# A means load over 128 partitions and long runs back from DRAM, in an attention kernel followed by a mixture of experts

## The chip, the cores and the metric

The kernel runs on one core of one Trainium2 chip. The metric is device time in microseconds. A profiled execution gives its own time, and beside it a span, from the first to the last instruction, with a record of every instruction and every DMA packet.

## The reference

Two parts, one after the other. The attention works on `q`, `k`, `v` of 8 batches, 8 heads, 576 positions and 64 features. The change sits in its first half, an attention between means of four neighbouring positions:

```python
q_d = q.reshape(B, H, Sd, factor, D).mean(axis=3)     # Sd = 144, factor = 4
k_d, v_d = ...                                        # likewise
out_d = sm_attn(q_d, k_d, v_d)                        # softmax attention, 144 x 144 a head
out_up = np.repeat(out_d, factor, axis=2)             # each row serves four positions
...
out_local = np.matmul(attn, v)                        # positions nearer than 4
return (out_up + out_local).astype(np.float32)
```

The result, as 4,608 tokens of 512 features, goes to a mixture of 16 experts in 4 groups: a group is chosen for a token, an expert in the group, and that expert's two layers (512 to 1,024, ReLU, back to 512) are applied and weighted.

## The kernel before

**Units.** The attention is done in 16 units. A unit is two heads of two batches: the two heads lie on partitions 0 to 63 and 64 to 127 of `q` and `k`, the two batches along the row. Values are laid out by the host in two forms: `vw`, windows of 42 positions for the local part, and `vm`, groups of four positions side by side for the means.

**Order.** All steps of all units are written out by hand in one long list (`ORDER`), and each engine runs its own instructions in that order. So a step that waits holds up everything behind it on the same engine. Most loads and the store and load of `odd` are issued on SP, in the order of the list; stores of `x` on ScalarE's queue.

**Means.** `pool_q` and `pool_k` add four positions of `q` and `k` (one VectorE reduction, or three GpSimd adds; the last letter of the step says which). `load_v` loads a unit's `vm` with two DMAs: 112 partitions with two chunks of 2 KB each (keys 0 to 111 of the one head, 32 to 143 of the other), and 64 partitions with one chunk (32 keys of each head). There are three buffers `vs`, and `clear vs i` sets partitions 64 to 111 of the third chunk to zero once. `pool_v` adds the four positions to `vd`.

**Attention of the means.** `s_down` multiplies `q` and `k` means into `b_d`, `s_down_exp` makes `Pd` of it, `turn_pd` transposes `Pd` on TensorE in three parts (by key chunk), `turn_pd_out` copies these to `PdT`, `out_down` multiplies by `vd`, `turn_down` turns the product back and `turn_down_out` divides by the sums, into `odn`.

**The way back through DRAM.** `down_store` writes `odn` to a DRAM buffer `odd` (two buffers), 512 bytes a row for two heads. `load_down` reads it back into 8 partitions of the window buffer `vw` of the unit, row `8l + r` to partition `2 + 15r`, place `l`: 256 bytes at a time. There these rows lie among the values of the windows, so that one multiplication in `x_bank` (L446) adds both halves of the attention. `turn_x`, `logits`, the router's steps and `store_x` follow.

**After the attention** the router's lists are finished, tokens are gathered, and the experts run one after another with weights that are loaded and split in the same rhythm, TensorE being the engine that sets it.

Of the kernel before, what the change touches and what calls it, by code (L numbers as in the profile page):

```python
# [9 lines left out]
F32 = mybir.dt.float32  # L10
# [4 lines left out]
ALU = mybir.AluOpType  # L15
AX = mybir.AxisListType
# [3 lines left out]
P = 128  # L20
B, H, S, D = 8, 8, 576, 64
SD = S // 4
G = 9
# [23 lines left out]
NATURAL = 2  # L47
HALVES = (slice(0, 5), slice(5, G))

KEYS = ((slice(0, 112), 112), (slice(112, 176), 64), (slice(176, 288), 112))  # L50

TILES = (slice(0, P), slice(160, 160 + P), slice(112, 176))

# [1 line left out]
class Attention:  # L55
# [9 lines left out]
    def __init__(self, tc, q, k, vm, vw, idf, xd, left, right, dram):  # L65
        nc = self.nc = tc.nc
        self.tc, self.q, self.k, self.vm_in, self.vw_in, self.idf = tc, q, k, vm, vw, idf
        cp = self.cp = left.enter_context(tc.tile_pool(name="attc", bufs=1))
        self.a1 = left.enter_context(tc.tile_pool(name="att1", bufs=1))
        self.a2 = left.enter_context(tc.tile_pool(name="att2", bufs=2))  # L70
        self.inp = right.enter_context(tc.tile_pool(name="inp", bufs=2, side="right"))
        self.odd = [dram.tile([320, P], F32, name=f"odd{i}") for i in range(2)]
        self.st, self.banks, self.lg = {}, {}, {}
        self.turns = 0
        self.xd = xd
        self.kt = [self.inp.tile([P, 2, S], F32, name=f"kt{i}", bufs=1) for i in range(3)]
        self.kz = [self.inp.tile([P, 2, 2, S + 6], F32, name=f"kz{i}", bufs=1) for i in range(2)]
        self.load_k(0)
        self.load_q(0)
        self.mask = self.inp.tile([P, G, W], BF16, name="mask", bufs=1)  # L80
        self.vw = [(cp if i < 2 else self.inp).tile([P, 2, 2 * NBLK, D], F32, name=f"vw{i}", bufs=1) for i in range(3)]
        self.warm = self.inp.tile([P, 4 * P], BF16, name="warm", bufs=1)
        nc.vector.memset(self.warm, 0.0)
        one = cp.tile([1, 1], F32, name="one")
        nc.gpsimd.memset(one, 0.0)
        nc.scalar.activation(one, one, AF.Exp)
        self.zero = cp.tile([P, 1], F32, name="zero")
        nc.gpsimd.memset(self.zero, 0.0)
        self.idb = cp.tile([P, P], BF16, name="idb")
        self.vd = [self.inp.tile([112, 3, 2, D], F32, name=f"vd{i}", bufs=1) for i in range(2)]  # L90
        self.vs = [self.inp.tile([112, 3, 2, 4 * D], F32, name=f"vs{i}", bufs=1) for i in range(3)]
        self.mg = [cp.tile([P, 5], F32, name=f"mg{i}") for i in range(2)]
        self.sg = [cp.tile([P, 5], F32, name=f"sg{i}") for i in range(2)]
        self.rg = [cp.tile([P, 6], F32, name=f"rg{i}") for i in range(2)]
        self.kept = {}
        for n, more, shape in (
            ("pt", 1, [P, G * P]), ("x", 2, [P, G, P]), ("PdT", 1, [112, 3, 2 * SD]), ("od", 1, [P, 2 * SD]), ("odn", 1, [P, 3, 2, D])
        ):
            self.kept[n] = [cp.tile(shape, F32, name=f"{n}0")] + [self.inp.tile(shape, F32, name=f"{n}{i + 1}", bufs=1) for i in range(more)]
        self.E = [cp.tile([P, G, WW, 3], F32, name=f"E{i}") for i in range(2)]  # L100
        self.shares = self.inp.tile([P, 8], F32, name="shares", bufs=1)
        self.xT = cp.tile([P, 27 * P // 2], F32, name="xT")
        self.edge = self.inp.tile([P, 3, W], F32, name="edge", bufs=1)
# [9 lines left out]
    def clear(self, what, i):  # L113

        memset = self.nc.gpsimd.memset
        if what == "E":
            for w, c in ((slice(0, LEAD), slice(0, 3)), (slice(LEAD + W, WW), slice(0, 3)), (slice(LEAD, LEAD + W), slice(2, 3))):
                memset(self.E[i][:, :, w, c], 0.0)
            self.nc.gpsimd.tensor_copy(self.E[i][:, :, 0:40:5, 2], self.shares.unsqueeze(1).to_broadcast([P, G, 8]))
        elif what == "kz":  # L120
            memset(self.kz[i][0:64, 1], 0.0)
            memset(self.kz[i][64:P, 0], 0.0)
            for c in (slice(0, 3), slice(3 + S, 6 + S)):
                memset(self.kz[i][:, :, :, c], 0.0)
        else:
            memset(self.vs[i][64:112, 2], 0.0)

    def masks(self):

# [63 lines left out]

    def load_v(self, u):
        vs = self.vs[u % 3].rearrange("p c b x -> p c (b x)")
        self.nc.sync.dma_start(out=vs[:, 0:2], in_=self.vm_in[u, :, 0:2])
        self.nc.sync.dma_start(out=vs[0:64, 2], in_=self.vm_in[u, 0:64, 2])

    def load_windows(self, u):

# [5 lines left out]
    def pool_q(self, u, eng):  # L206
        s = self.st[u]
        s["qd"] = self.inp.tile([P, 2 * SD], F32, tag="qd", name=f"qd{u}")
        x = s["qT"].rearrange("p b (s t) -> p (b s) t", t=4)
        if eng == "D":  # L210
            self.nc.vector.tensor_reduce(out=s["qd"], in_=x, axis=AX.X, op=ALU.add)
        else:
            self.add4(s["qd"], [x[:, :, t] for t in range(4)])

    def add4(self, o, x):
        nc = self.nc
# [92 lines left out]
    def s_down(self, u):  # L309
# [18 lines left out]
        for h, r in enumerate(hs):  # L328
            for b in range(2):
                o = rest[64 * h + 32 * b : 64 * h + 32 * b + 32]  # L330
                q = qd[r, 112 + 32 * b : 144 + 32 * b]
                if h == 0:
                    mm(o, q, kd[r, b])
                else:
                    mm(o[:, 0:112], q, kd[r, b, 32:])
                    mm(o[:, 112:], q, kd[r, b, :32])

    def s_down_max(self, u):
        V = self.nc.vector
# [31 lines left out]

    def turn_pd(self, u, kc):

        pt = self.bank(("pd", kc), u, [P, 2 * SD + P])
        lo = KEYS[kc][0].start
        pd = self.st[u]["Pd"]
        tr = self.nc.tensor.transpose
        if kc == 1:
            tr(pt[:, 2 * SD :], pd[:, 4, SD - P :], self.idf)
        else:  # L380
            o = 112 - 32 * kc
            tr(pt[:112, o : o + P], pd[:, 4, 0:112], self.idf)
        for b in range(2):
            n = P if kc == 1 else 112
            tr(pt[:n, 160 * b : 160 * b + P], pd[:, 2 * b : 2 * b + 2].rearrange("p h s -> p (h s)")[:, lo : lo + n], self.idf)

    def turn_pd_out(self, u, kc, eng):
        s = self.st[u]
        s["PdT"] = self.of("PdT", u)
        pt = self.banks.pop((("pd", kc), u))  # L390
        o = s["PdT"][:, kc]
        if kc == 1:
            two = lambda x: x.rearrange("p (b s) -> p b s", b=2)[:, :, 0:P]
            self.evac(eng, two(s["PdT"][:64, kc : kc + 2].rearrange("p k s -> p (k s)")[:, 0:320]), two(pt[:64, 0:320]))
            for h in range(2):
                self.evac(eng, o[32 * h : 32 * h + 32, 112:176], pt[96:, 2 * SD + 64 * h : 2 * SD + 64 * h + 64])
        else:
            self.evac(eng, o, pt[:112, 0 : 2 * SD])

    def out_down(self, u):  # L400
        nc = self.nc
        vd, pdt = self.vd[u % 2], self.st[u]["PdT"]
        pt = self.bank("od", u, [P, 2, SD])
        for r, kc, o in ((slice(0, 112), 0, 0), (slice(0, 112), 2, 64), (slice(0, 32), 1, 0), (slice(32, 64), 1, 64)):
            for b in range(2):
                nc.tensor.matmul(
                    pt[o : o + 64, b], vd[r, (0, 2, 1)[kc], b], pdt[r, kc, SD * b : SD * b + SD], start=(kc != 1 and b == 0), stop=(kc == 1), skip_group_check=True
# [22 lines left out]

    def down_store(self, u, q):

        o, d = self.of("odn", u).rearrange("p c h d -> p c (h d)"), self.odd[u % 2]
        self.queue(q).dma_start(out=d.rearrange("(c p) d -> p c d", c=2)[0:P], in_=o[:, 0:2])
        self.queue(q).dma_start(out=d[P:160], in_=o[16:48, 2])

    def load_down(self, u, q):

        self.queue(q).dma_start(out=self.windows(u)[2:ROWS:15][0:8], in_=self.odd[u % 2][0 : 2 * SD].rearrange("(l r) (h d) -> r h l d", r=8, h=2))

    def x_bank(self, u, i):
        pt = self.bank(("x", i), u, [P, 3, P])
# [773 lines left out]


ORDER = """
shared_rows; warm_up 12; masks; masks_out A; clear_windows 0; load_k 1; clear E 1; s_local 0 1; pool_q 0 D; pool_k 0 D; clear E 0; load_q 1
s_local 0 0; s_local_out 0 1; quarter_sum; clear vs 0; s_local_out 0 0; load_k 2; load_q 2; pool_q 1 P; load_v 0; s_down 0; warm_up 6  # L1220
s_down_max 0; s_local_exp 0 1; s_down_exp 0 0; s_local_exp 0 0; s_down_exp 0 2; s_down_exp 0 1; pool_q 2 D; pool_k 1 D; s_local 1 1
s_local_out 1 1; s_local 1 0; spread 2 0 A; spread 2 1 P; clear kz 0; pool_v 0; clear kz 1; clear vs 2; clear vs 1; pool_k 2 P; turn_pd 0 0
s_local_out 1 0; soft_local_sum 0 D; turn_pd 0 2; load_k 3; turn_pd 0 1; turn_pd_out 0 1 A; turn_pd_out 0 0 A; soft_local 0
turn_pd_out 0 2 A; s_down 1; s_local_exp 1 0; out_down 0; s_local_exp 1 1; turn_e 0 0; s_down_max 1; turn_e 0 2; s_down_exp 1 0
soft_down 0 D; s_down_exp 1 1; s_down_exp 1 2; clear_windows 1; load_windows 0; turn_e 0 1; out_down_out 0 D; soft_local_sum 1 D
turn_e_out 0 2 A; s_local 2 1; s_local_out 2 1; load_q 3; constants; load_k 4; s_local 2 0; spread 3 0 A; spread 3 1 P; turn_e_out 0 0 A
# [207 lines left out]
```

## Time and profile before

| what | value |
| --- | --- |
| runs (three): lowest, median, highest | 739.65, 745.89, 752.54 us |
| profiled execution: its own time | 742.23 us |
| its span | 740.3 us |
| mean granted TensorE clock | 0.975 |
| TensorE (PE) busy, share of the span | 696.6 us, 94% |
| VectorE (DVE), ScalarE (ACT), GpSimd (POOL) busy | 460.4, 388.1, 254.8 us |
| DMA | 144.94 MB, mean 196 GB/s |

A busy engine is one with an instruction in it; TensorE's matmuls are pipelined, so busy does not mean at its peak. The busy shares are means over two very different stages, the attention and the experts, so stretches are to be read one by one. A wait is put down to what came last, and an instruction that waits holds up its engine's queue.

### The profile page before, as it was taken

The page shows a single profiled execution, that of the slowest core. Times are in us where ns is not written, and L with a number is a line of the kernel's source. Part 1 is how long each engine was busy: PE and PEld are TensorE (multiplying, and loading weights), DVE is VectorE, ACT ScalarE, POOL GpSimd, SP SyncE. Part 2 cuts the span into 40 slices and gives each one's busy share as a digit, 9 for nine tenths or more (in the row PEclk, how much of TensorE's full clock was granted, in tenths as well). Part 3 has the DMA queues.
Part 4 walks back from the last instruction along what each step waited for, and adds up shares of the span by engine and source line. Part 5 has one row for each costly group of instructions (what it writes and reads, how often), then busy time and mean ns, then how long its engine had stood idle before and what let it go on. Part 6 is the DMA issues. An engine that isn't in the chain of part 4 may idle for free. (4 is left out here: it accounts for less than half of the span.)

```text
span 740.3 us, 17944 instructions
## 1 busy us (share of the span) xinstructions
PE 696.6 (94%) x7135; PEld 627.9 (85%) x7135; DVE 460.4 (62%) x821; ACT 388.1 (52%) x830; POOL 254.8 (34%) x301
## 2 busy tenths in 40 slices
PE   7789987988986989999999999999999999999997
PEld 4666766766765868998999999999999999999996
DVE  5777987979984756654445555464555555565641
ACT  6767744857674316653444444454554554555531
POOL 7956655558634732002211120312203213212211
PEclk7889998999999999999999999999999999999999
DMA  9979899999978456846554555556655665656600
GB/s 292 250 176 238 259 265 240 237 234 272 234 212 234 114 176 207 273 131 197 156 171 143 166 188 172 191 158 204 188 172 191 212 198 189 226 186 203 222 27 26
DMA packets 109911, 144.94 MB, mean 196 GB/s; under 512 B 22736, under 2 KB 78544, under 8 KB 109824
## 3 DMA queue, kind: packets, MB, share of 16 engines
q1 hardware_dynamic: 85216, 113.25, 52.7%
q0 software_dynamic: 7088, 21.66, 8.5%
q10 hardware_dynamic: 17520, 8.85, 4.9%
q8 instruction: 57, 0.93, 0.5%
q14 instruction: 30, 0.25, 0.1%
HBM read 122.43 MB, written 22.29 MB: 195 GB/s over the span
## 5 line engine op out<-in xcount | busy, mean ns | idle before, releaser
L885 PE MATMUL ph<-xh,w1h 128*128 128x256 f32 (+13 forms) x512 | 161.1, 316 | 0.0
L856 POOL DMA_INDIRECT xg<-xd,gi x47 | 48.6, 1034 | 323.0 <-ACT yo L959 290.3
L885 PE MATMUL ph<-xl,w1h 128*128 128x256 f32 (+13 forms) x512 | 156.1, 306 | 0.0
L885 PE MATMUL ph<-xh,w1l 128*128 128x256 f32 (+13 forms) x512 | 156.0, 307 | 0.0
L844 DVE TENSOR_TENSOR w2l<-raww,w2h 128x1024 fp32r<-128x1024 f32 x61 | 74.6, 1224 | 73.7 <-ACT w2h L843 63.3
L933 PE MATMUL y<-hl,w2h 128*128 128x416 f32 (+11 forms) x384 | 115.3, 311 | 0.0
L933 PE MATMUL y<-hh,w2l 128*128 128x416 f32 (+11 forms) x384 | 114.3, 308 | 0.0
L843 ACT ACTIVATE w2h<-raww 128x1024 fp32r<-128x1024 f32 x64 | 67.6, 1058 | 73.5 <-PE y L933 54.0
L885 PEld LDWEIGHTS ph<-xh,w1h 128*128 128x128 f32 x512 | 96.2, 188 | 1.4 <-issue 0.2
L885 PEld LDWEIGHTS ph<-xl,w1h 128*128 128x128 f32 x512 | 96.3, 188 | 0.9
L844 DVE TENSOR_TENSOR w1l<-raww,w1h 128x1024 fp32r<-128x1024 f32 x60 | 73.4, 1224 | 38.1 <-ACT w1h L843 32.8
L885 PEld LDWEIGHTS ph<-xh,w1l 128*128 128x128 f32 x512 | 96.2, 188 | 0.3
L890 DVE SCALAR_TENSOR_TENSOR hl<-ph,hh 128x256 fp32r<-128x256 f32 (+13 forms) x128 | 60.3, 476 | 55.5 <-ACT hh L889 52.6
L889 ACT ACTIVATE hh<-ph 128x256 fp32r<-128x256 f32 (+13 forms) x128 | 53.9, 422 | 71.9 <-PE ph L885 65.9
L933 PE MATMUL y<-hh,w2h 128*128 128x416 f32 (+11 forms) x384 | 87.7, 312 | 0.0
L843 ACT ACTIVATE w1h<-raww 128x1024 fp32r<-128x1024 f32 x64 | 67.6, 1058 | 31.0 <-PE ph L885 24.2
L933 PEld LDWEIGHTS y<-hh,w2l 128*128 128x128 f32 x384 | 72.3, 188 | 0.1
L933 PEld LDWEIGHTS y<-hl,w2h 128*128 128x128 f32 x384 | 72.2, 188 | 0.1
L960 POOL DMA_INDIRECT out_dram<-yo,oi x47 | 47.9, 1020 | 65.5 <-ACT yo L959 51.9
L933 PEld LDWEIGHTS y<-hh,w2h 128*128 128x128 f32 x384 | 62.9, 188 | 0.1
L446 PE MATMUL b_x<-vw,pt 126*32 126x128 f32 x1152 | 40.9, 285 | 9.5 <-DMA vw<-odd 5.1
L865 ACT ACTIVATE xh<-xt 128x256 fp32r<-128x256 f32 (+14 forms) x68 | 27.0, 420 | 39.8 <-PE xt L872 39.8
(227 smaller groups left out, 1289.0 us busy)
## 6 DMA issues: line engine op xcount, KB each, us to landing
raww<-in_moe_w_dram SPq DMA_DIRECT2D x128, 512.0 KB
vw<-in_vw_dram SPq DMA_DIRECT2D x32, 378.0 KB
kt<-in_k_dram SPq DMA_DIRECT2D x16, 576.0 KB
qT<-in_q_dram SPq DMA_DIRECT2D x16, 576.0 KB
xd<-x ACTq DMA_DIRECT2D x15, 576.0 KB
vs<-in_vm_dram SPq DMA_DIRECT2D x16, 448.0 KB
vw<-odd SPq DMA_DIRECT2D x16, 144.0 KB
vs<-in_vm_dram SPq DMA_DIRECT2D x16, 128.0 KB
```

The source lines that it names most:

```text
L446: self.nc.tensor.matmul(pt[32 * j : 32 * j + 32, t], self.of("pt", u)[:ROWS, 32 * lin : 32 * lin + 32], self.windows(u)[:ROWS, :, lin], st ...
L843: self.nc.scalar.activation(hi, raw, AF.Copy)
L844: eng.tensor_tensor(out=lo, in0=raw, in1=hi.bitcast(F32), op=ALU.subtract)
L856: self.nc.gpsimd.indirect_dma_start(out=xg[:w], out_offset=None, in_=self.xd[0:rows], in_offset=bass.IndirectOffsetOnAxis(ap=st["gi"][:w, ...
L865: self.nc.scalar.activation(hi, x, AF.Copy)
L885: nc.tensor.matmul(ph, a[:, k, cs], st[b][:, k], start=(n == 0), stop=(n == 11))
L889: nc.scalar.activation(hh, ph, AF.Relu)
L890: nc.vector.scalar_tensor_tensor(out=hl, in0=ph, scalar=0.0, in1=hh.bitcast(F32), op0=ALU.max, op1=ALU.subtract)
L933: nc.tensor.matmul(y, a[:, f % 2, cs], b, start=(f == 0 and n == 0), stop=(f == 7 and n == 2))
L960: i = nc.gpsimd.indirect_dma_start(out=self.out, out_offset=bass.IndirectOffsetOnAxis(ap=oi, axis=0), in_=yo[:m], in_offset=None, bounds_c ...
```

## The change

The means' keys are cut differently: keys 0 to 127 of the one head and 16 to 143 of the other in the two large chunks, so that the first load fills 128 partitions, and 16 keys of each head in the small one, loaded to partitions 48 to 79. The buffers `vs`, `vd` and `PdT` get 128 partitions. The third chunk of `vs` is now cleared as a whole, before anything is loaded, and these clears stand earlier in the order; the copy `quarter_sum` takes the place of two of them. The host lays out `vm` as two contiguous blocks a unit. `turn_pd` makes one transpose more for the middle part, `s_down` needs one multiplication where it took two for the second head. `pool_q` writes its means in the order batch, row within a block, block, instead of batch, block, row; the rows of `odd` then come in that order, with one head after the other, and `load_down` reads runs of 18 rows (4,608 bytes) instead of single ones of 256 bytes. `down_store` writes 256 bytes a row and head, with three DMAs instead of two.

The core of the diff (the sizes of buffers and the indices that follow from the new cut are left out):

```diff
-KEYS = ((slice(0, 112), 112), (slice(112, 176), 64), (slice(176, 288), 112))
+FIRST = (0, 80, 160)
+MAIN = P * 2 * 8 * D
...
-        self.odd = [dram.tile([320, P], F32, name=f"odd{i}") for i in range(2)]
+        self.odd = [dram.tile([2, 2 * SD, D], F32, name=f"odd{i}") for i in range(2)]
...
-            memset(self.vs[i][64:112, 2], 0.0)
+            memset(self.vs[i][:, 2], 0.0)
...
-        self.nc.sync.dma_start(out=vs[:, 0:2], in_=self.vm_in[u, :, 0:2])
-        self.nc.sync.dma_start(out=vs[0:64, 2], in_=self.vm_in[u, 0:64, 2])
+        self.nc.sync.dma_start(out=vs[:, 0:2], in_=self.vm_in[u, 0:MAIN].rearrange("(p c x) -> p c x", p=P, c=2))
+        self.nc.sync.dma_start(out=vs[48:80, 2], in_=self.vm_in[u, MAIN:].rearrange("(p x) -> p x", p=32))
...
-        x = s["qT"].rearrange("p b (s t) -> p (b s) t", t=4)
+        o = s["qd"].rearrange("p (b r k) -> p b r k", b=2, r=8)
+        x = s["qT"].rearrange("p b (k r t) -> p b r k t", r=8, t=4)
         if eng == "D":
-            self.nc.vector.tensor_reduce(out=s["qd"], in_=x, axis=AX.X, op=ALU.add)
+            self.nc.vector.tensor_reduce(out=o, in_=x, axis=AX.X, op=ALU.add)
         else:
-            self.add4(s["qd"], [x[:, :, t] for t in range(4)])
+            self.add4(o, [x[:, :, :, :, t] for t in range(4)])
...
-                if h == 0:
-                    mm(o, q, kd[r, b])
-                else:
-                    mm(o[:, 0:112], q, kd[r, b, 32:])
-                    mm(o[:, 112:], q, kd[r, b, :32])
+                mm(o, q, kd[r, b])
...
         if kc == 1:
-            tr(pt[:, 2 * SD :], pd[:, 4, SD - P :], self.idf)
+            tr(pt[:, 224 : 224 + P], pd[:, 4, 0:P], self.idf)
+            tr(pt[:, 352 : 352 + P], pd[:, 4, SD - P :], self.idf)
...
-        o, d = self.of("odn", u).rearrange("p c h d -> p c (h d)"), self.odd[u % 2]
-        self.queue(q).dma_start(out=d.rearrange("(c p) d -> p c d", c=2)[0:P], in_=o[:, 0:2])
-        self.queue(q).dma_start(out=d[P:160], in_=o[16:48, 2])
+        o, d = self.of("odn", u), self.odd[u % 2]
+        for c in range(2):
+            self.queue(q).dma_start(out=d[:, 160 * c : 160 * c + P].rearrange("h p d -> p h d"), in_=o[:, c])
+        self.queue(q).dma_start(out=d[:, P:160].rearrange("h p d -> p h d"), in_=o[16:48, 2])
...
-        self.queue(q).dma_start(out=self.windows(u)[2:ROWS:15][0:8], in_=self.odd[u % 2][0 : 2 * SD].rearrange("(l r) (h d) -> r h l d", r=8, h=2))
+        t = self.windows(u)[2:ROWS:15][0:8].rearrange("p h (b k) d -> p (h b) (k d)", b=2)
+        self.queue(q).dma_start(out=t, in_=self.odd[u % 2].rearrange("h (b r k) d -> r (h b) (k d)", b=2, r=8))
...
-shared_rows; warm_up 12; masks; masks_out A; clear_windows 0; load_k 1; clear E 1; s_local 0 1; pool_q 0 D; pool_k 0 D; clear E 0; load_q 1
-s_local 0 0; s_local_out 0 1; quarter_sum; clear vs 0; s_local_out 0 0; load_k 2; load_q 2; pool_q 1 P; load_v 0; s_down 0; warm_up 6
+shared_rows; warm_up 12; masks; clear vs 0; masks_out A; clear_windows 0; load_k 1; clear E 1; s_local 0 1; pool_q 0 D; pool_k 0 D
+clear E 0; clear vs 1; clear vs 2; load_q 1; s_local 0 0; s_local_out 0 1; s_local_out 0 0; load_k 2; load_q 2; pool_q 1 P; load_v 0
...
-s_local_out 1 1; s_local 1 0; spread 2 0 A; spread 2 1 P; clear kz 0; pool_v 0; clear kz 1; clear vs 2; clear vs 1; pool_k 2 P; turn_pd 0 0
+s_local 1 1; s_local_out 1 1; s_local 1 0; spread 2 0 A; spread 2 1 P; clear kz 0; pool_v 0; clear kz 1; quarter_sum; pool_k 2 P
...
-    laid["vm"] = _np.stack([mean[:, 0:112], mean[:, 176:288], mean[:, 112:224]], axis=2)
+    main = _np.stack([mean[:, 0:P], mean[:, 160:288]], axis=2)
+    laid["vm"] = _np.concatenate([x.reshape(4 * NB, -1) for x in (main, mean[:, P:160])], axis=1)
```

## Rows read from the trace of the kernel before

**Rows 1.** stretches: us, engines' busy us (instructions), granted clock, DMA share, GB/s

```profile
0.00:220.00 220.00, 191.56 (x3574) 143.43 (x3575) 177.92 (x390) 146.12 (x430) 138.74 (x199) 0.94 0.93 243
...
300.00:700.00 400.00, 400.00 (x2779) 393.91 (x2778) 220.56 (x304) 197.52 (x316) 78.22 (x77) 1.00 0.59 188
```

**Rows 2.** TensorE's waits, 0 to 226 us: total us, times, longest us

```profile
PE b_s L265 <- ACT Pd L353: 5.8, 5, 3.7
PE b_x L446 <- DMA vw<-odd: 5.1, 2, 2.9
```

**Rows 3.** timeline, TensorE and ScalarE, 112 to 120 us: start, us, what, idle before

```profile
118.18 0.48 PE L265 MATMUL b_s<-mask,idb 128*128 128x380 bf16 x1 [3.68 <-ACT Pd L353]
...
116.27 0.49 ACT L166 ACTIVATE x<-b_x 128x384 f32<-128x384 f32 x1 [4.08 <-DMA xd<-x]
```

**Rows 4.** table of stretches, around the stall at 113 us

```profile
113.00:118.00 5.00, 1.50 (x23) 1.10 (x21) 0.86 (x1) 1.64 (x7) 4.53 (x7) 0.89 0.83 226
117.00:124.00 7.00, 5.82 (x86) 4.43 (x85) 6.56 (x14) 4.79 (x17) 4.46 (x5) 0.52 1.00 268
```

**Rows 5.** DMA view, 4 to 10 us: loads of k and q alone

```profile
DMA packets 583, 2.39 MB, mean 399 GB/s; under 512 B 64, under 2 KB 64, under 8 KB 583
...
q1 hardware_dynamic: 583, 2.39, 100.2%
```

**Rows 6.** DMA view, 45 to 46 us: a means load almost alone

```profile
DMA packets 108, 0.34 MB, mean 340 GB/s; under 512 B 13, under 2 KB 13, under 8 KB 108
```

**Rows 7.** DMA view, 11 to 15 us: a means load among others

```profile
DMA packets 309, 1.03 MB, mean 257 GB/s; under 512 B 41, under 2 KB 41, under 8 KB 309
```

**Rows 8.** DMA view, 23 to 27 us: a means load among others

```profile
DMA packets 282, 0.86 MB, mean 214 GB/s; under 512 B 41, under 2 KB 41, under 8 KB 282
```

**Rows 9.** DMA view, 43 to 44 us: odd's load alone (40 slices)

```profile
DMA  0000000000000000003344544655475565645644
...
DMA packets 267, 0.07 MB, mean 68 GB/s; under 512 B 267, under 2 KB 267, under 8 KB 267
...
q1 hardware_dynamic: 267, 0.07, 29.4%
```

**Rows 10.** DMA view, 84 to 85 us: store of odd alone

```profile
DMA packets 139, 0.06 MB, mean 57 GB/s; under 512 B 28, under 2 KB 139, under 8 KB 139
...
q1 hardware_dynamic: 139, 0.06, 21.8%
```

**Rows 11.** DMA view, 214 to 215 us: a store of 16 bytes a run

```profile
DMA packets 783, 0.01 MB, mean 13 GB/s; under 512 B 783, under 2 KB 783, under 8 KB 783
...
q1 hardware_dynamic: 783, 0.01, 36.1%
```

**Rows 12.** waits of SP's queue, 0 to 226 us

```profile
SPq L439 <- DMA odd<-odn: 34.9, 12, 7.5
```

**Rows 13.** timeline of SP's queue, 30 to 48 us

```profile
33.45 0.41 SPq L435 DMA_DIRECT2D odd<-odn  x1
...
41.99 0.69 SPq L439 DMA_DIRECT2D vw<-odd  x1
```

**Rows 14.** timeline, GpSimd, 0 to 120 us

```profile
4.76 0.31 POOL L119 COPY E<-shares 128x72 f32<-128x72 f32 x1
...
5.90 0.94 POOL L551 COPY quarters<-idf 32x32 f32<-32x32 f32 x4
...
9.55 0.69 POOL L217 TENSOR_TENSOR qd<-qT 128x288 f32<-128x288 f32 x1 [2.13 <-DMA qT<-in_q_dram]
...
22.19 0.99 POOL L126 MEMSET vs<- 48x512 f32 x2
```

**Rows 15.** timeline, TensorE, 0 to 60 us

```profile
30.37 0.38 PE L385 MATMUL b_pd<-idf,Pd 128*112 128x128 f32 x2
...
33.27 1.16 PE L316 MATMUL b_d<-kd,qd 64*128 64x144 f32 x20
```

**Rows 16.** instructions on qd: duration ns min/median/max

```profile
L218 POOL TENSOR_TENSOR qd<-qd,qT x9: 934/952/1458, 10.3 to 178.5; 128x288 f32<-128x288 f32 x9
```

More of the change, by code (lines that the diff above doesn't have):

```diff
@@ L89, in __init__ @@
         self.idb = cp.tile([P, P], BF16, name="idb")
-        self.vd = [self.inp.tile([112, 3, 2, D], F32, name=f"vd{i}", bufs=1) for i in range(2)]
-        self.vs = [self.inp.tile([112, 3, 2, 4 * D], F32, name=f"vs{i}", bufs=1) for i in range(3)]
+        self.vd = [self.inp.tile([P, 3, 2, D], F32, name=f"vd{i}", bufs=1) for i in range(2)]
+        self.vs = [self.inp.tile([P, 3, 2, 4 * D], F32, name=f"vs{i}", bufs=1) for i in range(3)]
         self.mg = [cp.tile([P, 5], F32, name=f"mg{i}") for i in range(2)]
@@ L96, in __init__ @@
         for n, more, shape in (
-            ("pt", 1, [P, G * P]), ("x", 2, [P, G, P]), ("PdT", 1, [112, 3, 2 * SD]), ("od", 1, [P, 2 * SD]), ("odn", 1, [P, 3, 2, D])
+            ("pt", 1, [P, G * P]), ("x", 2, [P, G, P]), ("PdT", 1, [P, 3, 2 * SD]), ("od", 1, [P, 2 * SD]), ("odn", 1, [P, 3, 2, D])
         ):
@@ L372, in turn_pd @@
     def turn_pd(self, u, kc):
-        pt = self.bank(("pd", kc), u, [P, 2 * SD + P])
-        lo = KEYS[kc][0].start
+        pt = self.bank(("pd", kc), u, [P, 2 * SD + 3 * 64])
+        lo = FIRST[kc]
         pd = self.st[u]["Pd"]
@@ L378, in turn_pd @@
         if kc == 1:
-            tr(pt[:, 2 * SD :], pd[:, 4, SD - P :], self.idf)
+            tr(pt[:, 224 : 224 + P], pd[:, 4, 0:P], self.idf)
+            tr(pt[:, 352 : 352 + P], pd[:, 4, SD - P :], self.idf)
         else:
             o = 112 - 32 * kc
-            tr(pt[:112, o : o + P], pd[:, 4, 0:112], self.idf)
+            tr(pt[:, o : o + P], pd[:, 4, 8 * kc : 8 * kc + P], self.idf)
         for b in range(2):
-            n = P if kc == 1 else 112
-            tr(pt[:n, 160 * b : 160 * b + P], pd[:, 2 * b : 2 * b + 2].rearrange("p h s -> p (h s)")[:, lo : lo + n], self.idf)
+            tr(pt[:, 160 * b : 160 * b + P], pd[:, 2 * b : 2 * b + 2].rearrange("p h s -> p (h s)")[:, lo : lo + P], self.idf)
     def turn_pd_out(self, u, kc, eng):
@@ L393, in turn_pd_out @@
             two = lambda x: x.rearrange("p (b s) -> p b s", b=2)[:, :, 0:P]
-            self.evac(eng, two(s["PdT"][:64, kc : kc + 2].rearrange("p k s -> p (k s)")[:, 0:320]), two(pt[:64, 0:320]))
+            self.evac(eng, two(s["PdT"][:, kc : kc + 2].rearrange("p k s -> p (k s)")[:, 0:320]), two(pt[:, 0:320]))
             for h in range(2):
-                self.evac(eng, o[32 * h : 32 * h + 32, 112:176], pt[96:, 2 * SD + 64 * h : 2 * SD + 64 * h + 64])
+                self.evac(eng, o[64 * h : 64 * h + 64, 112:176], pt[64 - 64 * h : P - 64 * h, 352 - 64 * h : 416 - 64 * h])
         else:
-            self.evac(eng, o, pt[:112, 0 : 2 * SD])
+            self.evac(eng, o, pt[:, 0 : 2 * SD])
     def out_down(self, u):
@@ L403, in out_down @@
         pt = self.bank("od", u, [P, 2, SD])
-        for r, kc, o in ((slice(0, 112), 0, 0), (slice(0, 112), 2, 64), (slice(0, 32), 1, 0), (slice(32, 64), 1, 64)):
+        for r, kc, o in ((slice(0, P), 0, 0), (slice(0, P), 2, 64), (slice(0, 64), 1, 0), (slice(64, P), 1, 64)):
             for b in range(2):
@@ L1218 @@
 ORDER = """
-shared_rows; warm_up 12; masks; masks_out A; clear_windows 0; load_k 1; clear E 1; s_local 0 1; pool_q 0 D; pool_k 0 D; clear E 0; load_q 1
-s_local 0 0; s_local_out 0 1; quarter_sum; clear vs 0; s_local_out 0 0; load_k 2; load_q 2; pool_q 1 P; load_v 0; s_down 0; warm_up 6
-s_down_max 0; s_local_exp 0 1; s_down_exp 0 0; s_local_exp 0 0; s_down_exp 0 2; s_down_exp 0 1; pool_q 2 D; pool_k 1 D; s_local 1 1
-s_local_out 1 1; s_local 1 0; spread 2 0 A; spread 2 1 P; clear kz 0; pool_v 0; clear kz 1; clear vs 2; clear vs 1; pool_k 2 P; turn_pd 0 0
-s_local_out 1 0; soft_local_sum 0 D; turn_pd 0 2; load_k 3; turn_pd 0 1; turn_pd_out 0 1 A; turn_pd_out 0 0 A; soft_local 0
+shared_rows; warm_up 12; masks; clear vs 0; masks_out A; clear_windows 0; load_k 1; clear E 1; s_local 0 1; pool_q 0 D; pool_k 0 D
+clear E 0; clear vs 1; clear vs 2; load_q 1; s_local 0 0; s_local_out 0 1; s_local_out 0 0; load_k 2; load_q 2; pool_q 1 P; load_v 0
+s_down 0; warm_up 6; s_down_max 0; s_local_exp 0 1; s_down_exp 0 0; s_local_exp 0 0; s_down_exp 0 2; s_down_exp 0 1; pool_q 2 D; pool_k 1 D
+s_local 1 1; s_local_out 1 1; s_local 1 0; spread 2 0 A; spread 2 1 P; clear kz 0; pool_v 0; clear kz 1; quarter_sum; pool_k 2 P
+turn_pd 0 0; s_local_out 1 0; soft_local_sum 0 D; turn_pd 0 2; load_k 3; turn_pd 0 1; turn_pd_out 0 1 A; turn_pd_out 0 0 A; soft_local 0
 turn_pd_out 0 2 A; s_down 1; s_local_exp 1 0; out_down 0; s_local_exp 1 1; turn_e 0 0; s_down_max 1; turn_e 0 2; s_down_exp 1 0
```

## The prediction

> **What bounds the kernel now.** I read the table of stretches first [rows 1]. From 300 to 700 us TensorE is busy in every microsecond of the 400, and the change touches nothing there; that part can only begin earlier or later. The attention, which the change edits, fills the first 220 us. There TensorE is busy 191.6 us, so 28.4 us of it are idle, and the DMA engines are busy for 0.93 of the time while they move only 243 GB/s. So two things press on this stage at once, and what it can win is some of those 28.4 us.
>
> Second, TensorE's waits in that stage [rows 2]. Two name the transfers: 5.1 us for `vw<-odd` (the rows that come back from DRAM), and the 3.7 us wait inside the 5.8 us for `Pd`. The second is a transfer in disguise, as the timeline of the two engines shows [rows 3]: the score matmuls of L265 stand still until 118.18 us for ScalarE's exponentials, and ScalarE itself had stood for 4.08 us until 116.27 us, because it could not overwrite `x` before an older store of it had landed. [...] Together 5.1 + 3.7 + 2.9 = 11.7 us: this is the ceiling of what faster transfers can give, if every transfer wait went. The rest of the idle time (the start, the clears on ScalarE, waits on VectorE) is not the transfers' and stays.
>
> Third, what a transfer costs. Loads of `k` and `q` alone run at 399 GB/s with all engines busy [rows 5]. A means load almost alone runs at 340 GB/s [rows 6]. Where it lies among other loads the engines are just as busy, but only 257 GB/s [rows 7] or 214 GB/s [rows 8] come through.
>
> **The means load (128 partitions).** It moves 576 KB (590 kB) a unit before and after, 448 + 128 KB then, 512 + 64 KB now. Time of a unit now: 590/340 = 1.73 us almost alone, 590/257 = 2.30 us and 590/214 = 2.76 us among others. If the new shape ran like `k` and `q`, it would take 590/399 = 1.48 us. The gain is thus between 0.25 and 1.28 us a unit. Below nothing: the small part now goes to 32 partitions, and the narrowest load in the trace, the rows to 8 partitions, makes 8 x 256 / 17.6 ns = 116 GB/s (worked out below) [rows 9]. At that the 65.5 kB take 0.56 us, and with the 524 kB at 340 (1.54 us) that is 2.10 us, a loss of 0.37 us against 1.73. I take a gain of 0.4 us, nearer to the lone row than to the crowded ones, since the crowd (window loads, the 512-byte stores of `x`) is not changed. 16 units: 6.4 us of all DMA engines' time; ends 5.9 us lost and 20.5 us gained.
>
> What speaks against a gain here is that a partition of the large part receives 4,096 bytes before and after, and one of the small part 2,048. [...]
>
> **The rows from DRAM.** Now one load is 576 runs of 256 bytes. A run costs 0.294 x 16 x 1,000 / 267 = 17.6 ns, and in the later slices about half of the 16 engines work [rows 9]; eight partitions, eight engines, 72 runs each: 1.27 us. After, an engine has 4 runs of 4,608 bytes. Such a run costs 1.002 x 16 x 6,000 / 519 = 185 ns, the 64 tiny packets of that view left out [rows 5]: 0.74 us. Gain 0.53 us of eight engines, 0.27 us of all, a unit; 4.3 us in all. If the runs were cut into small ones again, nothing.
>
> The store pays. 288 runs of 512 bytes become 576 of 256, and two issues become three. A stored run of 512 bytes costs 0.218 x 16 x 1,000 / 139 = 25 ns, 31 if the 28 tiny ones cost nothing [rows 10]. No row stores 256 bytes: the nearest are a stored run of 16 bytes, 0.361 x 16 x 1,000 / 783 = 7.4 ns [rows 11], and a loaded one of 256, 17.6 ns. I take 17.6 (same size; the 16-byte store shows that a short store is not dear in itself): 576 x 17.6 / 16 = 0.63 us against 288 x 28 / 16 = 0.50, so +0.13 us. Ends: 7.4 ns, -0.24 us; 31 ns, the price of a run twice as long, +0.62 us. 16 units: +2.1 us (-3.8 to +9.9).
>
> [...]
>
> **The queue.** SP issues the load behind the stores, and waits for them at its head: 34.9 us in 12 waits [rows 12]. In unit 0 the second store was issued at 33.45 us and the load went out at 41.99, and until then SP could issue nothing else: the means loads, `k`, `q` and windows behind it wait too [rows 13]. The third store adds one issue of 0.41 us (that of the second, in the same rows) and 0.13 us of writing ahead of that wait, the load itself gives 0.53 us back. Net for the chain store, load, L446: nothing.
>
> **What costs nothing, and its cover.** GpSimd: the clear of `vs` 0 moves ahead of the clears of `E`, those of `vs` 1 and 2 ahead of the first `qd` add, which now begins at 9.55 us after 2.13 us of waiting for `qT`; the two (0.99 us) fit there, while the copy of `quarters` (0.94 us) leaves that place and takes theirs at 22.19 us [rows 14]. Without that cover it would be 1 us once. A clear of 128 partitions costs what one of 48 does, since it has the same 512 elements in a row. The small means load of unit 0 now waits for that clear, on SP, some 0.3 us; nothing is queued behind it until 9.07 us. TensorE: one transpose more a unit, at most 0.38/2 = 0.19 us (two in 0.38 us), and four matmuls in `s_down` become two, 2 x 1.16/20 = 0.12 us less [rows 15]: at most 16 x 0.07 = 1 us, in a stage with 28 us idle. Evacuations and means keep their elements a partition; taller operands (128 for 112, 64 for 32 rows) change no length. `pool_q` reads with a step of 128 bytes instead of 16. Nine of 16 are on GpSimd, three adds each. Bounds: nothing, as elements are the same; or the price of the copy into `E`, whose runs are as short, 0.31 us for 72 elements, 4.3 ns each [rows 14], which would make 1.24 us of an add that now takes 0.95 [rows 16]: 27 x 0.29 = 8 us. GpSimd is idle 81 of the 220 us [rows 1], so I take nothing.
>
> **Sum.** DMA work a unit: -0.4 - 0.27 + 0.13 = -0.54 us, 8.6 us in all, of 0.93 x 220 = 205 us. The slack of the DMA engines goes from 7 to 11%. I estimate that time spent waiting in a line goes with one over its slack, so about 1 - 7/11 = 0.36, say 0.4, of the 11.7 us should go: 4.7 us. What goes next to the front is TensorE's own order: it is busy 87% of this stage already, and waits on the other engines remain. The profiled execution took 742.23 us (740.3 span, 1.9 around it): 737.5. The runs' median is 745.89, with 739.65 and 752.54 as the others; on that scale 741.2. I write 739.5, between the two.
>
> **Rivals.** *No gain:* the means load is as fast as its bytes a partition, its term is nothing, and 4.3 - 2.1 = 2.2 us of DMA work are left, a slack of 8% and 0.12 of 11.7 us: 1.4 us, 741 (744.5 on the median's scale). For it: 340 GB/s alone. Against: 214 and 257 among others. That the long runs don't come about, or that the strided adds eat them, ends in the same place, 742. *All of it:* the crowded rows are the means load's own doing, the term is +20 us, slack 17%, and the waits and the slow clock go: -11.7, 730.5. Against: `x` stores and window loads crowd too. *Slower:* SP's head of line. If stored runs of 256 bytes cost what 512 do, each unit holds SP 0.41 + 0.62 = 1.03 us longer, and everything queued behind starts that much later: 16.5 us over 16 units. With the same share reaching TensorE as above, 0.4, it is +6.6 us, 749. It decides from the point where the stores grow by more than the 0.53 us that the load saves.
>
> **How the numbers follow.** Forecast 0.47; no gain 0.29; all of it 0.12; slower 0.12. The forecast's own range is 2 to 9 us less (733 to 740, up to 744 on the median's scale). Runs of one kernel here spread by 13 us, so a difference below 2% is about what a measurement cannot tell from none, and the range reaches to 730 and to 750. Faster by over 2% means below 731: 0.10, the best half of "all of it" and some spread. Slower by over 2% means above 760.8: 0.03. Within: 0.87.
>
> **What would show it.** Right: the share of DMA time over the first 220 us falls below 0.9; windows with a means load show well over 257 GB/s; the rows' load goes from 576 packets to a few dozen of 4,608 bytes; `vw<-odd` nearly leaves TensorE's waits; and the expert stage begins 4 to 5 us earlier. Wrong: the same 214 to 257 GB/s in those windows; more than 34.9 us of SP waiting for `odd`; GpSimd adds on `qd` over 1.2 us; or an attention that shortens its waits and gets others in their place, since each engine keeps to its written order.

## The result and the profile after

The changed kernel takes 734.99 us (median of 6 runs, 733.48 to 737.93); beside it the kernel before took 745.72 (6 runs, 739.65 to 757.93). The ratio is 0.9859 [0.9819, 0.9900]: faster, by less than 2%. The profiled execution took 734.79 us with a span of 732.8, against 742.23 and 740.3. The forecast was 739.5 with a range of 730 to 750. It expected 4.7 us less; the medians lie 10.7 us apart, the profiled executions 7.4. On two other chips, below, the medians lie 11.2 and 6.1 us apart. The ratios leave out every run more than 1.5% above the fastest of its kernel, which on the chip of the first four experiments takes 15 of the 35 runs of before (the median of the rest is 740.13 us, not 742.91) and none of the others', so that those four ratios lie 0.4 to 0.6% above the ratios of the medians.

Where did the time go? First the end of the attention: the last matmul of L446 starts at 237.4 us before and at 228.8 after. The table of stretches up to these points, before and then after (us, busy us of TensorE, weight load, VectorE, ScalarE and GpSimd with their instructions, granted clock, DMA share, GB/s); the fence of after also has the stretches that answer [rows 1] and [rows 4]:

```profile
0.00:237.40 237.40, 203.41 (x3766) 152.03 (x3770) 186.09 (x411) 152.25 (x443) 144.58 (x203) 0.94 0.92 243
...
30.00:40.00 10.00, 7.22 (x108) 5.67 (x108) 8.29 (x18) 9.12 (x26) 9.46 (x10) 1.00 1.03 250
```

```profile
0.00:228.80 228.80, 202.05 (x3721) 148.60 (x3722) 186.44 (x411) 152.16 (x444) 145.37 (x203) 0.95 0.85 253
...
0.00:220.00 220.00, 195.27 (x3633) 144.09 (x3634) 184.18 (x406) 148.60 (x437) 140.68 (x201) 0.96 0.85 253
...
300.00:700.00 400.00, 400.00 (x2788) 393.29 (x2787) 219.49 (x307) 196.45 (x318) 78.69 (x77) 1.00 0.57 184
...
30.00:40.00 10.00, 8.73 (x95) 6.67 (x96) 5.23 (x12) 7.77 (x24) 9.39 (x11) 0.66 0.71 228
...
113.00:118.00 5.00, 4.49 (x99) 3.32 (x100) 4.86 (x10) 3.45 (x8) 4.69 (x6) 1.00 0.98 313
117.00:124.00 7.00, 6.85 (x152) 5.21 (x148) 6.14 (x16) 5.51 (x22) 2.08 (x3) 1.00 1.13 270
```

Up to its end, the attention has 237.4 - 203.41 = 34.0 us without TensorE before and 228.8 - 202.05 = 26.75 after: 7.2 us of idle time and 1.4 us of busy time are gone, together the 8.6 us. What follows takes 502.9 us before and 504.0 after, so 7.5 us are left at the end. In this profile the stall at 113 us and the slow clock behind it [rows 4] are gone: TensorE is busy 4.49 of those 5 us at clock 1.00. The slow clock is not gone from the kernel for good: in the second profile of the changed kernel (below) the same 5 us have a mean clock of 0.50, with TensorE busy 4.55 us, and in all three of its profiles 30 to 40 us have 0.66, where before has 1.00. Meanwhile the DMA share went from 0.92 to 0.85 although the rate rose.

TensorE's waits (total us, times, longest us), the answer to [rows 2]:

```profile
PE b_pd L377 <- ACT pt L167: 3.7, 1, 3.7
PE b_d L318 <- DVE E L290: 3.1, 4, 1.8
...
PE b_s L267 <- ACT Pd L351: 2.2, 4, 0.9
...
PE b_x L446 <- DMA vw<-odd: 2.0, 1, 2.0
```

`vw<-odd` fell from 5.1 to 2.0 us and the wait for `Pd` from 5.8 to 2.2. Of the 6.7 us, some came back: `b_pd` for ScalarE's `pt` stood at 2.0 us before and `b_d` for `E` at 2.4, and they are 2.4 us longer. Those are waits between engines, no longer transfers: ahead of the 3.7 us wait, ScalarE is busy for 4.07 us (from 25.37 us) clearing a window buffer.

The DMA view of 11 to 15 us, of 23 to 27 us, and of 43.2 to 44.6 us, where the stores of `odd` run alone:

```profile
DMA packets 403, 1.44 MB, mean 360 GB/s; under 512 B 59, under 2 KB 59, under 8 KB 403
...
DMA packets 396, 1.39 MB, mean 348 GB/s; under 512 B 52, under 2 KB 52, under 8 KB 396
...
DMA packets 544, 0.13 MB, mean 94 GB/s; under 512 B 544, under 2 KB 544, under 8 KB 544
...
q1 hardware_dynamic: 544, 0.13, 44.8%
```

Where a means load lies among others, 360 and 348 GB/s come through instead of 257 and 214 [rows 7, 8], with engines no busier than before (q1 103.0 and 100.4%, against 104.1 and 103.7). This is the clearest difference between the two traces. A stored run of 256 bytes takes 0.448 x 16 x 1,400 / 544 = 18.4 ns.

SP's queue, its waits and then the timeline of unit 0, which answer [rows 12, 13]:

```profile
SPq L433 <- DVE odn L424: 40.3, 12, 6.4
SPq L439 <- DMA odd<-odn: 20.6, 16, 4.3
...
32.37 0.42 SPq L434 DMA_DIRECT2D odd<-odn  x1
...
36.09 0.70 SPq L439 DMA_DIRECT2D vw<-odd  x1
```

The wait for the stores to land fell from 34.9 to 20.6 us, while SP's wait for VectorE to write `odn`, ahead of the first store, is 40.3 us and was 25.6 before: a part of what SP gained it waits in another place. In unit 0 the load goes out 3.7 us behind the last store instead of 8.5 (its 0.41 us issue included). That what the stores queue behind drains faster would explain it; this is not shown.

### The profile page after: what moved, and what is told of

It is laid out like the page before. It is cut to its first block, busy times and chain, and to the rows that moved or that the text cites. A ratio compares the mean times of both kernels' runs of the same rounds, so it can differ in the third digit from the quotient of the medians.

```text
span 732.8 us, 17877 instructions
## 1 busy us (share of the span) xinstructions
PE 695.7 (95%) x7086; PEld 624.5 (85%) x7087; DVE 460.7 (63%) x821; ACT 387.1 (53%) x830; POOL 254.3 (35%) x301
## 5 line engine op out<-in xcount | busy, mean ns | idle before, releaser
L885 PE MATMUL ph<-xh,w1h 128*128 128x256 f32 (+13 forms) x512 | 161.1, 316 | 0.0
L446 PE MATMUL b_x<-vw,pt 126*32 126x128 f32 x1152 | 39.5, 282 | 3.9 <-DMA vw<-odd 2.0
```

Source lines behind the costliest of these rows:

```text
L446: self.nc.tensor.matmul(pt[32 * j : 32 * j + 32, t], self.of("pt", u)[:ROWS, 32 * lin : 32 * lin + 32], self.windows(u)[:ROWS, :, lin], st ...
L885: nc.tensor.matmul(ph, a[:, k, cs], st[b][:, k], start=(n == 0), stop=(n == 11))
```

## The experiments

Two theories. The first: the gain is the means load's, because its large part now fills 128 partitions; as a variant, because its two parts are now contiguous blocks of DRAM. The second: it is the long runs of the rows, and the shorter chain of store, load and L446. One measure serves all of them: the time in packets of SP's queue (q1) up to the last matmul of the attention, as its share of that stretch. For before and after (queue: packets, MB, share):

```profile
q1 hardware_dynamic: 33289, 47.63, 75.3%
```

```profile
q1 hardware_dynamic: 29470, 47.91, 67.6%
```

0.753 x 237.4 = 178.8 us before, 0.676 x 228.8 = 154.7 after: 24.1 us less of all engines' time. The queue of the `x` stores (q10) hardly changes: 0.151 x 237.4 = 35.8 us and 0.156 x 228.8 = 35.7. Repeats of a kernel differ by 1 to 5 us in this measure, so a difference of that size says little.

**The cut alone.** The changed kernel with the path of `odd` as before:

```
-        self.odd = [dram.tile([2, 2 * SD, D], F32, name=f"odd{i}") for i in range(2)]
+        self.odd = [dram.tile([320, P], F32, name=f"odd{i}") for i in range(2)]
...
-            self.add4(o, [x[:, :, :, :, t] for t in range(4)])
+            self.add4(s["qd"], [x[:, :, t] for t in range(4)])
...
+        self.queue(q).dma_start(out=d.rearrange("(c p) d -> p c d", c=2)[0:P], in_=o[:, 0:2])
+        self.queue(q).dma_start(out=d[P:160], in_=o[16:48, 2])
...
+        self.queue(q).dma_start(out=self.windows(u)[2:ROWS:15][0:8], in_=self.odd[u % 2][0 : 2 * SD].rearrange("(l r) (h d) -> r h l d", r=8, h=2))
```

> The new cut of the means alone (128 partitions, contiguous blocks, the moved clears); the rows come back from DRAM as before, in 256-byte runs. Theory 1 (the means load took more of the DMA engines' time than its bytes, and slowed the loads beside it): most of the gain is here, 0.988 to 0.991 of before, DMA share of the first 220 us from 0.93 to about 0.87. Rival (the long runs shorten the chain of store, load and L446): 0.996 to 1.000 here.

736.32 us (12 runs), before 742.91: ratio 0.9950 [0.9906, 0.9993], the medians' own 0.9911. Its DMA view of 11 to 15 us, and its q1 to the attention's end, at 232.1 us:

```profile
DMA packets 397, 1.42 MB, mean 355 GB/s; under 512 B 57, under 2 KB 57, under 8 KB 397
...
q1 hardware_dynamic: 33024, 47.62, 69.4%
```

Nearly the whole rise in rate is the cut's. q1 has 0.694 x 232.1 = 161.1 us, 17.7 less than before. The packet records of the two traces split this: packets of 2,048 and 4,096 bytes, which are the means loads' but for 512 of them, fell from 42.6 to 31.0 us, and those of 4,608 bytes, the loads of `k`, `q` and windows beside them, from 105.8 to 100.2.

**The long runs alone.** The kernel before with the four edits above turned round, so with `odd`, `pool_q`, the stores and the load of the changed kernel.

> The long runs alone: the order of the q means, the new layout of odd, three stores, one load of 4,608-byte runs; the means load stays on 112 and 64 partitions. Theory 1: 0.996 to 1.000 of before, DMA share still above 0.9, means packets still slow among others. Rival (the chain through DRAM): 0.988 to 0.991, and the wait of L446 for vw<-odd (5.1 us) gone.

739.72 us (12 runs): 1.0006 [0.9965, 1.0047], the medians' own 0.9957. The same two rows, the second to 238 us:

```profile
DMA packets 322, 1.08 MB, mean 271 GB/s; under 512 B 42, under 2 KB 42, under 8 KB 322
...
q1 hardware_dynamic: 29458, 47.64, 72.0%
```

q1 has 171.4 us, 7.4 less than before; its repeat, in the last experiment, 3.6 less. In these profiles the two parts add up, 17.7 + 7.4 = 25.1 against 24.1 for the whole, closer than the repeats of one kernel mostly agree. The long runs bring no time by themselves that is clear of the noise. Why not, the last experiment asks.

**Contiguous blocks, old cut.** The kernel before, with the two parts of 112 and 64 partitions laid one behind the other in DRAM:

```
-        self.nc.sync.dma_start(out=vs[:, 0:2], in_=self.vm_in[u, :, 0:2])
-        self.nc.sync.dma_start(out=vs[0:64, 2], in_=self.vm_in[u, 0:64, 2])
+        self.nc.sync.dma_start(out=vs[:, 0:2], in_=self.vm_in[u, 0:MAIN].rearrange("(p c x) -> p c x", p=112, c=2))
+        self.nc.sync.dma_start(out=vs[0:64, 2], in_=self.vm_in[u, MAIN:].rearrange("(p x) -> p x", p=64))
```

> The kernel before, with only the host's layout changed: the 112 x 4,096 bytes of a unit, and the 64 x 2,048, lie in one piece in DRAM, instead of with a pitch of 6,144 bytes. Theory 1a (it is the partitions that a DMA writes): 0.997 to 1.003 of before, the stretches with a means load stay near 214 to 257 GB/s. Rival 1b (it is the contiguous source): 0.989 to 0.993, and those stretches near 300 GB/s or more.

744.10 us (10 runs): 1.0078 [1.0032, 1.0123], the medians' own 1.0016. From 11 to 15 us:

```profile
DMA packets 309, 1.04 MB, mean 260 GB/s; under 512 B 39, under 2 KB 39, under 8 KB 309
```

260 GB/s against 257: the variant of the first theory falls. The 0.8% in the ratio is no slowdown that the medians bear out: they are 744.10 and 742.91.

**Two halves of 64 partitions.** The changed kernel, same bytes to the same places, with one issue more a unit:

```
-        self.nc.sync.dma_start(out=vs[:, 0:2], in_=...)
+        for r in (slice(0, 64), slice(64, P)):
+            self.nc.sync.dma_start(out=vs[r, 0:2], in_=...[r])
```

> The changed kernel, with the large means load cut into two DMAs of 64 partitions each (same bytes, same runs, same contiguous source, one issue more on SP a unit). Theory 1a (what counts is how the partitions of one DMA fall on the engines): the means load is slow again, 4,096-byte packets 1.3 to 2 times as long, and the time goes back by half or more of the gain: 0.991 to 0.998 of before. Rival 1c (a load is fast when all 128 partitions get the same, in whatever pieces): 0.984 to 0.988, as the changed kernel.

741.71 us (10 runs): 1.0045 [0.9994, 1.0096], the medians' own 0.9984. From 11 to 15 us, and q1 to 231.6 us:

```profile
DMA packets 279, 0.88 MB, mean 220 GB/s; under 512 B 58, under 2 KB 58, under 8 KB 279
...
q1 hardware_dynamic: 29440, 47.62, 76.2%
```

q1 is back at 176.5 us. Neither a partition's 4,096 bytes nor the addresses differ from the changed kernel, only how many partitions one DMA covers (and one issue more). The moved clears and the contiguous blocks are kept too, so they are not what gives the rate. The packet records show it most directly. Only the large part of the means load comes in packets of 4,096 bytes, and up to the end of the attention one of them takes, in the median, 264 ns before, 254 with contiguous blocks, 251 and 264 with the long runs alone (112 partitions each), 286 in halves of 64, and 160 to 164 ns in every kernel that loads 128 partitions at once. In time it stands with the long runs under the old cut (739.72 on the same chip). Part of its loss can be the extra issue, by the price that the last experiment gives. Its profiled execution, 738.63 us, is at the low end of its runs, and its attention ends at 231.6 us, 5.8 earlier than before with nearly the same q1: q1 is a measure of the transfers, and the time doesn't follow it closely.

**No means loads.** Before and after with the means loads of units 3 to 15 left out, two issues a unit with them, beside the changed kernel again:

```
     def load_v(self, u):
+        if u >= 3:
+            return
```

> The changed kernel once more, beside the others on one chip. If the two parts simply add (new cut alone 0.995, long runs alone 1.0006): 0.994 to 0.997 of before. If the long runs only pay once the means load is out of the way: 0.984 to 0.989, as first measured.

> The kernel before without the means loads of units 3 to 15 (they use the values of the first three units; 13 of 16 loads are left out). Theory 1 (the means load, by its own time and by slowing others, is what the new cut takes away): DMA work of the attention falls by 30 us or more, and the time to 0.980 to 0.990 of before. Rival (the new cut gains by something other than transfers): 0.995 to 1.000.

> The changed kernel without the means loads of units 3 to 15 (same values left out). Theory 1: little is left in these loads, 0.980 to 0.986 of before, within 0.5% of the changed kernel. Rival 1d (the DMA engines still set the pace of the attention): 0.970 to 0.978.

The later units use the values of the first three instead, so tokens can be routed otherwise; behind the attention TensorE has 3,377 matmuls in each of the traces. On this chip before took 744.32 us. The changed kernel: 733.10, 0.9828 [0.9786, 0.9869]. Before without the loads: 732.06, 0.9823 [0.9776, 0.9870]. After without them: 733.41, 0.9829 [0.9779, 0.9879]. q1 of the last two, to 229.3 and 226.0 us:

```profile
q1 hardware_dynamic: 30663, 40.04, 60.5%
```

```profile
q1 hardware_dynamic: 26687, 39.95, 59.2%
```

The means loads, and what they do to their neighbours, thus hold 178.8 - 138.7 = 40.1 us before, 3.1 a unit, and 154.7 - 133.8 = 20.9 after, 1.6 a unit, for the same bytes. By the medians before gains 12.3 us without them, the 26 issues included; the changed kernel gains nothing more, although its attention then ends 2.8 us earlier (226.0 us against 228.8), as what follows takes longer (505.7 us against 504.0).

**Stores twice.** The changed kernel with each store of `odd` made a second time, to a tile that nothing reads: three issues and 576 runs of 256 bytes more a unit.

```
+        for d in (self.odd_more[u % 2], self.odd[u % 2]):
```

> The changed kernel with every store of the means' rows made a second time, ahead of the first, into a DRAM buffer that nobody reads: three issues on SP and 576 runs of 256 bytes more a unit, ahead of the load that waits. If SP's head of line is what decides (the slower rival): 3 x 0.41 + 0.63 = 1.9 us a unit, 30 us, of which 0.4 or more reach the end: 12 us or more, 1.000 to 1.01 of before. If a short store is as cheap as reckoned and covered: 0.985 to 0.992.

745.99 us (10 runs): 1.0019 [0.9988, 1.0050], 12.9 us above the changed kernel on that chip. The gain is gone. SP's waits:

```profile
SPq L435 <- DVE odn L425: 16.6, 10, 3.9
SPq L441 <- DMA odd<-odn: 10.5, 9, 2.6
```

SP's waits for `odn` and `odd` shrank from 40.3 + 20.6 to 27.1 us: its spare time was filled.

**Three issues that move next to nothing.** The changed kernel with three stores of 16 x 16 bytes ahead of the real ones, beside the changed kernel and each part again:

```
+        for c in range(3):
+            self.queue(q).dma_start(out=self.odd_more[u % 2][0, 16 * c : 16 * c + 16, 0:4], in_=o[0:16, 0, 0, 0:4])
```

> The changed kernel, now on one chip with both halves of the change. 0.981 to 0.988 of before, as twice before.

> The new cut alone, again. If the parts add (each takes DMA work away, and the time follows the DMA work at about half a microsecond a microsecond): 18 us of DMA work less, 0.986 to 0.991. If the first reading holds and the long runs are needed for the rest: 0.993 to 0.998.

> The long runs alone, again. If the parts add: 8 us of DMA work less, 0.993 to 0.997. If the first reading holds: 0.998 to 1.003, because the third store's issue on SP eats the shorter load.

> The changed kernel with three more store issues a unit ahead of its own, as in the kernel with doubled stores, but each of them only 16 runs of 16 bytes. If the price of the doubled stores (from 0.983 to 1.002) lies in SP's issues and the order of its queue: 3 x 0.41 us a unit, 20 us on SP, 0.990 to 1.000. If it lies in the data (576 runs of 256 bytes a unit, 11 us of DMA work): 0.982 to 0.988.

Before took 742.35 us on this chip. The changed kernel: 736.24, 0.9921 [0.9895, 0.9947]. The cut alone: 737.08, 0.9930 [0.9902, 0.9958]. The long runs alone: 743.17, 1.0008 [0.9973, 1.0042]. With the three issues: 744.82, 1.0035 [1.0002, 1.0068], so 8.6 us for 48 tiny DMAs, more than the 1.000 at the upper end of what was expected. The changed kernel missed its 0.981 to 0.988 here: its gain was 11.2 us on the last chip and is 6.1 on this one. q1 in the repeats, in the order changed kernel (above, to 229.5 us), changed kernel (here, to 228.9), cut alone (to 235.0), long runs alone (to 238.1):

```profile
q1 hardware_dynamic: 29170, 47.60, 69.6%
```

```profile
q1 hardware_dynamic: 29183, 47.62, 68.5%
```

```profile
q1 hardware_dynamic: 33160, 47.76, 68.9%
```

```profile
q1 hardware_dynamic: 29450, 47.63, 73.6%
```

That is 159.7, 156.8, 161.9 and 175.2 us: 19.1, 22.0, 16.9 and 3.6 less than before. The tile that the 48 DMAs write to (ns least/median/most of an issue), and SP's waits:

```profile
L435 SPq DMA_DIRECT2D oddm<-odn x48: 303/412/1844, 31.0 to 225.0; - x48
...
SPq L435 <- DVE odn L425: 19.0, 10, 3.3
SPq L443 <- DMA odd<-odn: 10.1, 9, 2.4
```

48 x 0.412 = 19.8 us of SP's time; 0.43 of it reaches the end. If they cost alike, an issue more a unit costs 8.6 / 3 = 2.9 us, so two thirds of what the doubled stores cost is their issues, if the chips compare. Of all kernels that do the whole work none here beats the changed one, but on this chip, the one that ran both, the cut alone equals it within the noise.

## Why the forecast came out as it did

The direction and the place, transfers in the attention, were right. The mechanism was right in part: the cut of the means load makes transfers shorter, but more, and for the reason that the forecast gave to a rival; the long runs, the other part of the forecast's saving, bring no time alone that is clear of the noise. That the time lies in the range is partly luck: 734.99 us is 4.5 us from the forecast's 739.5 and 4.5 from that rival's 730.5.

- **The means load** was mis-sized. Forecast 6.4 us of DMA work (ends -5.9 and +20.5); the cut alone took 17.7 us off q1, 16.9 in its repeat. The step that failed is the choice of 0.4 us a unit, nearer to the lone row [rows 6] than to the crowded ones [rows 7, 8], on the reason that the crowd itself isn't changed. The crowded rows were mostly the means load's own doing: with 128 partitions the same crowd runs at 360 and 348 GB/s, at which 590 kB take 1.64 and 1.70 us instead of 2.30 and 2.76. The rows themselves spoke against the crowd's part: in both, as many packets are under 512 B as under 2 KB (41), so not one 512-byte store of `x` was in that crowd. That the bytes of a partition set the time is refuted by the halves (286 ns a packet against 160, at the same 4,096 bytes).
- **The long runs** were sized at -4.3 + 2.1 = -2.2 us of DMA work; alone they took 7.4 and 3.6 us off q1, no clear miss given how far repeats differ. The store was right: 18.4 ns a run for 17.6 taken, under the 25 to 31 of a 512-byte run [rows 10], so +0.16 us a unit for +0.13. The load may have been a little low: its price was taken from a stretch where it ran alone, 17.6 ns a run [rows 9], and by the packet records of the whole attention before, where only this load has packets of 256 bytes, one took 21 ns on the mean. After, it is 32 packets of 4,608 bytes a unit, as forecast.
- **The share that reaches the end.** With the DMA slack of 0.15 in the first 220 us, the rule of one over the slack (the prediction's estimate, which no run tests) gives 1 - 7/15 = 0.53 of 11.7 us, 6.2 us. Measured were 7.5 between profiles and 10.7, 11.2 and 6.1 between medians: the last is about that, the others are more. Of the ceiling's three terms, the wait for `odd` gave 3.1 of 5.1 us, the wait for `Pd` 3.6 for 3.7, the slow clock at most the 1.4 us of TensorE's busy time for 2.9, since among others a slow stretch came at 30 us for the one that went. That was the last of the prediction's signs of being wrong, waits that others replace, and it came in part. The 2.9 us, half of TensorE's 5.8 busy us at a mean clock of 0.52 [rows 4], no run shows as a saving of its own. In its place the traces show what the same work takes at either clock: nine matmuls into `b_e` 2.16 us at 0.50 (before, from 120.03 us) and 1.17 at 1.00 (after, from 111.87), forty of 128x76 into `b_s` 1.50 (before, from 118.58) and 0.86 (after, from 110.47).
- **The rivals.** "No gain" fell with the 360 GB/s. "All of it" (the crowd is the means load's own doing, 730.5) named the true cause; between medians its -11.7 is nearer than the forecast's -4.7, between profiled executions -7.4 is nearer to the forecast. "Slower" had a real mechanism, as added issues do cost time: 0.43 of theirs reaches the end. That this is near the 0.4 taken is chance, since the 0.4 was worked out from the DMA engines' slack.
- **Net nothing for the chain** of store, load and L446 came out, as the long runs alone make no difference clear of the noise, twice over (1.0006 and 1.0008; by the medians 0.9957 and 1.0011). That the third issue, 2.9 us by the last experiment, is what eats their saved DMA work fits the numbers; a kernel with the long runs and two issues was not tried, so it is argued, not shown. How much the long runs add on top of the cut stays open: 0.8 us between medians on the last chip, the only one that ran both. In the profiles the attention ends earlier with both (228.8, 229.5 and 228.9 us) than with the cut alone (232.1 and 235.0), and at 238.0 and 238.1 with the long runs alone; but what follows takes from 499.8 to 505.7 us in these seven profiles, so several of these microseconds can be lost again behind the attention, and no run tells why.
- **What was costed at nothing** stayed there. GpSimd's timeline after, and its adds on `qd` (ns least/median/most), beside [rows 14, 16]:

```profile
3.96 0.53 POOL L127 MEMSET vs<- 128x512 f32 x1
...
6.33 1.02 POOL L127 MEMSET vs<- 128x512 f32 x2
9.43 0.68 POOL L219 TENSOR_TENSOR qd<-qT 128x288 f32<-128x288 f32 x1 [2.08 <-DMA qT<-in_q_dram]
...
L220 POOL TENSOR_TENSOR qd<-qd,qT x9: 932/948/1538, 10.2 to 168.4; 128x288 f32<-128x288 f32 x9
```

The clears fit ahead of the first add, which begins at 9.43 us instead of 9.55 and still waits 2.08 us for `qT`. The step of 128 bytes costs nothing: 948 ns against 952 for an add. Nor did taller operands take longer, by more than some ns: a clear of 128 partitions 529 ns for 520 with 48, an add into `vd` 1,002 over 128 partitions and over 112 (medians), 16 products with `vd` 1.36 us with 128 rows (from 108.91 us) and with 112 (from 113.14).

## What to carry to other kernels

When loads run at a lower rate wherever one of them takes part, with the engines just as busy, suspect that load's shape before the crowd, and try it spread over all 128 partitions in one DMA: here 360 GB/s came through from 11 to 15 us, against 257 with 112 partitions and 220 with two halves of 64. Leave the load out once to see how much there is to win at all: here 12 us before, nothing after. Profile a kernel twice before reading a few microseconds out of one trace. On a queue whose head waits for landings count issues as well as bytes; here 0.4 us of added issuing cost 0.18 us at the end, which by the numbers can eat a better transfer.

## What the runs showed of the hardware

- In these runs the rate of a stretch with a means load went with the partitions that one DMA covers. From 11 to 15 us, with about the same neighbours: 220 GB/s with halves of 64, 231 to 271 with 112, 348 to 360 with 128 (the repeats of each kernel included), at 4,096 bytes a partition each time and with the engines always busy (q1 alone 101 to 107%). The packets beside the means load slow down as well: one of 4,608 bytes takes 178 ns where `k` and `q` run alone (median, 4 to 10 us before), and from 11 to 15 us 271 to 348 with 112 partitions, 384 with halves, 187 to 221 with 128. Why a packet took longer with fewer partitions no run here tells.
- DMAs of 256 bytes cost SP 0.412 us each, and 48 of them made the kernel 8.6 us slower; yet taking 26 issues and their loads out of the changed kernel gave nothing (733.41 against 733.10). So a price of an issue was measured for added ones alone; what sets the time below the present number no run here shows.
